# Gate and up weights streamed in memory order, with the column shuffle moved into the block transposes

## The chip, the cores and the metric

The kernel runs on one NeuronCore of a Trainium2 chip. TensorE (PE) multiplies matrices and writes PSUM; its weight loads are shown apart as PEld. VectorE (DVE) and ScalarE (ACT) do the elementwise work, GpSimd (POOL) prepares constants, and SyncE (SP) issues nearly all DMAs from HBM. The metric is device time in microseconds (us), as the median of several executions. A profile is one further execution with the hardware profiler on.

## The reference, cut to what matters

A decode step for four tokens, with attention over a sliding window and a SwiGLU block, both fed by the same layer-normed input and added to the residual:

```
x = A_x                                   # [4, 1, 512] bf16
xn = layernorm(x)
q = (xn @ wq)                             # 32 heads of 128
k, v = last 4096 rows of the caches       # 4 batches x 8 kv heads, each used by 4 query heads
attn = softmax(q k^T / sqrt(128)) v @ wo
ffn  = (silu(xn @ w_gate) * (xn @ w_up)) @ w_down     # 512 -> 1792 -> 512
out = x + attn + ffn
```

Only the two products with `w_gate` and `w_up` (512 x 1792 each) and what reads them are touched by the change.

## The kernel before, in words

All five engines run programs written out by hand, each in its own block of the source, and they meet only at semaphores; no scheduler moves anything. The order on each engine is the order of its block.

SP issues the loads on one queue: `wq`, two K tiles, `w_gate`, `w_up`, and then in turn a V tile and a K tile (2 MB each) as their buffers come free. Sixteen steps (`ND`) cover the cache, each with two batches' halves of one kv head. After the last K tile come `w_down`, the last V tile in two halves with semaphores of their own (`d_v[1]` and `d_vz`), and then `wo` in four pieces cut at 16, 26, 30 and 32 blocks (`WO_CUTS`). `w_gate` and `w_up` have been in SBUF since the start.

PE transposes K through PSUM, multiplies it with q, applies the softmax shift, and multiplies P with V; DVE evacuates the transposes and finds the row maxima. That is the loop. After the loop PE does, in this order: the second half of the last-but-one P times V (`pv(0, 1, ...)`), the last softmax shift, **the gate and up products (L443 to L449 of the source)**, the residual (`I4w` times `X`), the last two halves of P times V (which wait for the two halves of V), the down projection (which waits for `guT` from DVE), four transposes of the attention output, a small product that regroups it (`rep`), and the output projection with `wo`, 64 matmuls which wait for the four pieces of `wo` at blocks 0, 16, 26 and 30. DVE casts the sum and SP and ACT each store half of it.

The gate and up products put the 4 tokens (padded to 32) on the output partitions. Each of the four 32-partition groups `j` of PSUM takes 448 of the 1792 columns, and four input chunks `c` are summed, so that each product is 16 matmuls: 4 sets of 4 matmuls, one per column group of the array. Column number `f` of the weight is `14*p + t`: `w_down` is loaded so that row `f` sits in partition `p`, block `t`. The matmuls of before read each group's columns with `t` outermost, that is one element every 14, so that the 448 results lie in PSUM as 14 runs of 32, ready for 32x32 blocks:

```
wv = w[:, c, :].rearrange("p (m t) -> p t m", t=NF)
mm(o[32*j:32*j+32, :].rearrange("p (t m) -> p t m", t=NF), XnT[:, c, :], wv[:, :, 32*j:32*j+32], ...)
```

DVE then transposes each product in 32x32 blocks from PSUM to SBUF (`gT` at L330, `uT` at L332), which puts `p` on the partitions. ACT takes exp of `-gT` (L265), DVE makes silu(gate) times up (L334 to L340) into `guT`, and the down projection reads that. `norm` (L310 to L314) of the last attention step comes behind `guT` on DVE.

All these matmuls are issued through the helper `mm`, so their line in the profile is L354, and they are told apart by their tensors.

Of the kernel before, what the change touches and what calls it, by code (L numbers as in the profile page):

```python
# [10 lines left out]
def bass_parallel_sum__sliding_block_cached__swiglu_ffn__decode_kernel(  # L11
# [10 lines left out]
    out: bass.AP,  # L22
):
    B, _, D = A_x.shape
    _, HKV, Sk, Dh = A_k_cache.shape
    HQ = A_wq.shape[1] // Dh
    F = B_w_gate.shape[1]
# [3 lines left out]
    NF = F // 128  # L31
# [49 lines left out]
    XnT = sb("xnT", [128, NC, 32], BF16)  # L81
# [7 lines left out]
    gT = WQ[:, 0:NF * 64].bitcast(FP32)  # L89
    uT = WQ[:, NF * 64:NF * 128].bitcast(FP32)  # L90
# [16 lines left out]
    gate_ps = ps_kt[0][:, 0:NF * 32]  # L107
    up_ps = ps_kt[1][:, 0:NF * 32]
# [3 lines left out]
    def sem(name):  # L112
        return nc.alloc_semaphore(name=name)
# [21 lines left out]
    s_gt = sem("s_gt")  # L135
# [35 lines left out]
    with nc.Block() as block:  # L171
# [97 lines left out]
        @block.vector  # L269
        def _(eng):  # L270
            eng.wait_ge(d_x, 16)
            eng.tensor_reduce(st_neg[:], X[:], AX.X, ALU.add, negate=True).then_inc(s_xc, 1)
            eng.wait_ge(s_ss, 1)
            eng.tensor_scalar(st_var[:], st_sum[:], 1.0 / D, EPS * D * D, ALU.mult, ALU.add).then_inc(s_var, 1)
            eng.wait_ge(s_std, 1)
            eng.reciprocal(st_rstd[:], st_std[:]).then_inc(s_rs, 1)
            eng.wait_ge(s_xT, 1)
            eng.wait_ge(s_const, 1)
            eng.tensor_copy(XnT[:, :, 0:B], xT_ps.rearrange("p (c b) -> p c b", b=B)).then_inc(s_xnT, 1)
            for n in range(2):  # L280
                eng.wait_ge(s_q, n + 1)
                eng.transpose(qT[:, 512 * n:512 * n + 512], ps_kt[n][:])  # L282
            eng.drain()
            for i in range(2):
                last = eng.tensor_copy(  # L285
                    QZ[:].rearrange("p (k i) c -> p k i c", i=2)[:, :, i, 0:C].rearrange("p k (m h) -> p k m h", m=2),
                    qT.rearrange("p (k h x) -> p k x h", h=REP, x=32)[:, :, 2 * i:2 * i + 2, :])
            last.then_inc(s_qz, 1)
            eng.engine_nop().then_inc(s_ev, NG)

            def evac(u, tr):
                for g in range(NG):
                    eng.wait_ge(s_tr, tr + g + 1)
                    eng.tensor_copy(KT[:, u * HKN + 1024 * g:u * HKN + 1024 * (g + 1)],  # L294
                                    kt_ps[g].rearrange("p a b -> p (a b)")).then_inc(s_ev, 1)

            def row_max(bank, n):
                eng.wait_ge(s_sc, n)
                eng.tensor_reduce(RM[:], ps_S[bank][:].rearrange("p (t c) -> p c t", c=C), AX.X,  # L299
                                  ALU.max).then_inc(s_rm, 1)  # L300

            def shift(n):
                eng.wait_ge(s_mt, n)
                eng.tensor_reduce(m8[:], mt_ps, AX.X, ALU.max)  # L304
                eng.drain()
                eng.tensor_scalar(Dg[:], I8[:], m8[:, 0:1], -1.0, ALU.mult, ALU.mult).then_inc(s_dg, 1)

            def norm(n, b, r):
                eng.wait_ge(s_pv, n)
                eng.tensor_reduce(den[:], den_ps.rearrange("p (t c) -> p c t", c=C), AX.X, ALU.add)  # L310
                eng.drain()
                eng.reciprocal(den[:], den[:])
                eng.drain()
                eng.tensor_tensor(OT[:, 2 * b:2 * b + 2, ds(r * REP, REP)],  # L314
                                  O_ps.rearrange("p (j h) -> p j h", j=2),
                                  den[:].rearrange("p (j h) -> p j h", j=2), ALU.mult).then_inc(s_nrm, 1)

            with eng.Fori(0, ND // 2) as r:
                for b in range(2):
                    row_max(1 - b, 2 * r + (b + 1))  # L320
                    evac(0, 4 * NG * r + 2 * NG * b)
                    shift(2 * r + (b + 1))
                    norm(2 * r + (b + 1), b, r)
                    evac(1, 4 * NG * r + (2 * NG * b + NG))
            row_max(1, ND + 1)
            shift(ND + 1)
            norm(ND + 1, 0, ND // 2)

            eng.wait_ge(s_gate, 1)
            eng.transpose(gT, gate_ps).then_inc(s_gt, 1)  # L330
            eng.wait_ge(s_up, 1)
            eng.transpose(uT, up_ps)  # L332
            eng.wait_ge(s_ex, 1)
            eng.tensor_scalar(ex[:], ex[:], 1.0, None, ALU.add)  # L334
            eng.drain()
            eng.reciprocal(ex[:], ex[:])
            eng.drain()
            eng.tensor_tensor(ex[:], gT.rearrange("p (t b) -> p t b", b=32)[:, :, 0:B], ex[:], ALU.mult)
            eng.drain()
            eng.tensor_tensor(guT[:], uT.rearrange("p (t b) -> p t b", b=32)[:, :, 0:B], ex[:],  # L340
                              ALU.mult).then_inc(s_guT, 1)
            norm(ND + 2, 1, ND // 2)

            eng.wait_ge(s_t4, 1)
            eng.tensor_copy(OB[:], tr_ps).then_inc(s_ob, 1)  # L345
            eng.wait_ge(s_pm, 1)
            eng.tensor_copy(OP[:].rearrange("p c b -> p b c"), op_ps.rearrange("p (b c) -> p b c", b=B)).then_inc(s_op, 1)  # L347
            eng.wait_ge(s_acc, 1)
            eng.tensor_copy(y[:], ps_acc[:, 0:256]).then_inc(s_y, 1)  # L349

        @block.tensor
        def _(eng):
            def mm(o, l, r, start=False, stop=True):
                return eng.matmul(o, l, r, start=start, stop=stop, skip_group_check=True)  # L354
# [3 lines left out]
            for c in range(NC):  # L358
                last = eng.transpose(xT_ps[:, c * B:(c + 1) * B],  # L359
                                     xn[:].rearrange("b (p c) -> b c p", c=NC)[:, c, :], I4[:])  # L360
# [4 lines left out]
            for n in range(2):  # L365
                for c in range(NC):
                    wv = WQ[:, c * HQ * Dh:(c + 1) * HQ * Dh].rearrange("p (n h d) -> p n h d", n=2, d=Dh)
                    for j in range(4):
                        last = mm(ps_kt[n][32 * j:32 * j + 32, :].rearrange("p (h d) -> p h d", d=32), XnT[:, c, :],
                                  wv[:, n, :, 32 * j:32 * j + 32], start=(c == 0))  # L370
# [72 lines left out]
            for w, o, done, d in ((WG, gate_ps, s_gate, d_wg), (WU, up_ps, s_up, d_wu)):  # L443
                eng.wait_ge(d, 16)
                for c in range(NC):
                    wv = w[:, c, :].rearrange("p (m t) -> p t m", t=NF)
                    for j in range(4):
                        last = mm(o[32 * j:32 * j + 32, :].rearrange("p (t m) -> p t m", t=NF), XnT[:, c, :],
                                  wv[:, :, 32 * j:32 * j + 32], start=(c == 0))  # L449
                last.then_inc(done, 1)  # L450
            for n in range(2):
                mm(ps_acc[64 * n:64 * n + 64, 0:256], I4w[:], X[:, 256 * n:256 * n + 256], start=True)
# [9 lines left out]
            for i in range(B):  # L462
                last = eng.transpose(  # L463
                    tr_ps[:, i, :],
                    OT[:, i, REP:], ident[:])
            last.then_inc(s_t4, 1)
            eng.wait_ge(s_ob, 1)
            for e in range(REP):
                last = mm(op_ps.rearrange("p (b c) -> p b c", b=B), rep[:, e, :], OB[:, :, 32 * e:32 * e + 32],
                          start=(e == 0))  # L470
            last.then_inc(s_pm, 1)
            eng.wait_ge(s_op, 1)
            for c in range(NO):
                if c in WO_CUTS:
                    eng.wait_ge(d_wo[WO_CUTS.index(c)], 16)
                for n in range(2):
                    last = mm(ps_acc[64 * n:64 * n + B, 0:256], OP[:, c, :], WO[:, c, 256 * n:256 * n + 256])
# [29 lines left out]
```

## Time and profile before

| what | value |
|---|---|
| median of 3 runs | 200.13 us (199.88 to 200.15) |
| the profiled execution | 200.16 us, of which the span from first to last instruction is 198.4 us |
| PE busy | 167.4 us (84%) |
| DVE busy | 115.6 us (58%) |
| ACT busy | 16.6 us (8%) |
| HBM read | 81.01 MB, 408 GB/s over the span |

The page gives busy times per engine and a chain of work that ended last, followed back from the last instruction. An element count such as 128x448 is partitions by elements. A "timeline" row is start, duration, engine, line and operation, output and input tensors, count, and in brackets the idle time before it and what ended it. The tensor names are the kernel's; gate and up are `ps_kt<-wg_sb,xnT` and `ps_kt<-wu_sb,xnT`, because they use two of the PSUM banks of the K transposes, and `gT` and `uT` lie in the space of `wq_sb`.

### The profile page before, as it was taken

The page shows a single profiled execution, that of the slowest core. Times are in us where ns is not written, and L with a number is a line of the kernel's source. Part 1 is how long each engine was busy: PE and PEld are TensorE (multiplying, and loading weights), DVE is VectorE, ACT ScalarE, POOL GpSimd, SP SyncE. Part 2 cuts the span into 40 slices and gives each one's busy share as a digit, 9 for nine tenths or more (in the row PEclk, how much of TensorE's full clock was granted, in tenths as well). Part 3 has the DMA queues.
Part 4 walks back from the last instruction along what each step waited for, and adds up shares of the span by engine and source line. Part 5 has one row for each costly group of instructions (what it writes and reads, how often), then busy time and mean ns, then how long its engine had stood idle before and what let it go on. Part 6 is the DMA issues. An engine that isn't in the chain of part 4 may idle for free.

```text
span 198.4 us, 7741 instructions
## 1 busy us (share of the span) xinstructions
PE 167.4 (84%) x3458; PEld 141.5 (71%) x3458; DVE 115.6 (58%) x250; ACT 16.6 (8%) x26; POOL 10.3 (5%) x23
## 2 busy tenths in 40 slices
PE   0137999749999989898989898989898998989975
PEld 0113898748988878787878797978787887873363
DVE  1004758545777767676666767575858575762430
ACT  5600010001010101010101010101010101011000
POOL 8920000000000000000000000000000000000000
PEclk9999999988999999999999999999999999999999
DMA  6999999999999999999999999999999999999950
GB/s 232 449 410 426 432 419 430 438 423 433 406 433 423 429 429 429 443 436 423 429 429 426 433 446 426 429 429 426 433 446 426 429 429 426 436 418 448 411 230 1
DMA packets 5934, 81.10 MB, mean 409 GB/s; under 512 B 668, under 2 KB 680, under 8 KB 936
## 3 DMA queue, kind: packets, MB, share of 16 engines
q1 hardware_dynamic: 5912, 81.01, 95.9%
q8 instruction: 5, 0.08, 0.1%
q10 hardware_dynamic: 16, 0.01, 0.0%
q14 instruction: 1, 0.01, 0.0%
HBM read 81.01 MB, written 0.00 MB: 408 GB/s over the span
## 4 chain that ended last, share of the span: by engine, by line
DMA 51%; PE 42%; DVE 3%; issue 2%; DVEq 0%
DMA kbuf<-in_A_k_cache_dram 45%; PE ps_kt L382 17%; PE ps_s L354 9%; PE ps_o L354 7%; DMA wq_sb<-in_A_wq_dram 6%; PE ps_kt L354 5%; PE ps_acc L354 4%; DVE kT L294 1%; DVE kT L282 0%; DVE rm L299 0%; DVE oP L347 0%; DVE y_sb L349 0%; DVE oB L345 0%; DVE qz L285 0%; PE ps_kt L463 0%
## 5 line engine op out<-in xcount | busy, mean ns | idle before, releaser
L294 DVE COPY kT<-ps_kt 128x1024 bf16<-128x1024 bf16 x128 | 80.1, 684 | 27.2 <-PE ps_kt L382 27.1
L382 PE MATMUL ps_kt<-ident,kbuf 128*128 128x128 bf16 x1024 | 65.6, 224 | 10.6 <-DMA kbuf<-in_A_k_cache_dram 10.5
L382 PEld LDWEIGHTS ps_kt<-ident,kbuf 128*128 128x128 bf16 x1024 | 59.9, 100 | 15.9 <-issue 15.9
L354 PE MATMUL ps_o<-p,vbuf 128*128 128x64 bf16 x1120 | 38.7, 194 | 0.0
L354 PEld LDWEIGHTS ps_o<-p,vbuf 128*128 128x128 bf16 x1120 | 35.5, 98 | 1.2
L354 PEld LDWEIGHTS ps_s<-qz,kT 128*128 128x128 bf16 x1024 | 31.4, 98 | 6.7 <-issue 3.7
L354 PE MATMUL ps_s<-qz,kT 128*128 x1024 | 34.7, 192 | 1.2
L263 ACT ACTIVATE p<-ps_s 128x512 bf16<-128x512 f32 x17 | 10.1, 597 | 162.2 <-PE ps_s L354 162.2
L299 DVE TENSOR_REDUCE rm<-ps_s 128x8 bf16<-128x512 f32 x17 | 11.8, 692 | 20.5 <-PE ps_s L354 20.5
L354 PE MATMUL ps_o<-p,ones 128*128 128x128 bf16 (+1 forms) x69 | 7.0, 222 | 2.3 <-DVE qz L285 1.3
L354 PE MATMUL ps_kt<-wq_sb,xnT 128*32 128x512 bf16 x32 | 3.6, 630 | 5.4 <-DMA wq_sb<-in_A_wq_dram 5.4
L354 PEld LDWEIGHTS ps_o<-p,ones 128*128 128x128 bf16 x69 | 4.5, 98 | 3.5 <-issue 2.2
L359 PE MATMUL ps_acc<-i,xn 4*128 4x4 f32 x4 | 0.6, 254 | 7.4 <-ACT xn L260 7.4
L354 PE MATMUL ps_s<-mkc,mkr 2*128 2x512 bf16 x17 | 6.8, 398 | 0.0
L354 PE MATMUL ps_s<-dg,ones 8*128 8x512 bf16 x17 | 6.5, 385 | 0.0
L354 PEld LDWEIGHTS ps_kt<-wq_sb,xnT 128*32 128x32 bf16 x32 | 1.3, 139 | 6.9 <-issue 6.9
L282 DVE STREAM_TRANSPOSE kT<-ps_kt 128x512 f32<-128x512 f32 x2 | 1.4, 716 | 8.1 <-PE ps_kt L354 8.1
L310 DVE TENSOR_REDUCE den<-ps_o 128x8 f32<-128x128 f32 x18 | 5.0, 276 | 1.4 <-PE ps_o L354 1.4
L359 PEld LDWEIGHTS ps_acc<-i,xn 4*128 4x128 f32 x4 | 0.6, 208 | 7.3 <-issue 7.3
L207 POOL MEMSET vbuf<- 128x6144 f32 x1 | 5.2, 5222 | 0.0
L304 DVE TENSOR_REDUCE m<-ps_acc 8x1 f32<-8x128 f32 x17 | 4.6, 268 | 0.3 <-PE ps_acc L354 0.3
L314 DVE TENSOR_TENSOR oT<-ps_o,den 128x8 f32 (+1 forms) x18 | 3.0, 167 | 2.9 <-issue 2.7
(65 smaller groups left out, 52.0 us busy)
## 6 DMA issues: line engine op xcount, KB each, us to landing
kbuf<-in_A_k_cache_dram SPq DMA_DIRECT2D x16, 2048.0 KB, 12.6
vbuf<-in_A_v_cache_dram SPq DMA_DIRECT2D x15, 2048.0 KB, 11.2
wq_sb<-in_A_wq_dram SPq DMA_DIRECT2D x1, 4096.0 KB, 12.4
vbuf<-in_A_v_cache_dram SPq DMA_DIRECT2D x2, 1024.0 KB, 9.2
wo_sb<-in_A_wo_dram SPq DMA_DIRECT2D x1, 2048.0 KB, 14.5
wg_sb<-in_B_w_gate_dram SPq DMA_DIRECT2D x1, 1792.0 KB, 25.7
wu_sb<-in_B_w_up_dram SPq DMA_DIRECT2D x1, 1792.0 KB, 29.3
wd_sb<-in_B_w_down_dram SPq DMA_DIRECT2D x1, 1792.0 KB, 15.0
```

The costliest lines, as they stand in the source:

```text
L207: eng.memset(VB[:, HKN:].bitcast(FP32), 0.0)
L263: eng.activation(P[:, d % 2 * PS:d % 2 * PS + SN], ps_S[d % 2][:], ACT.Exp, scale=SCALE).then_inc(s_p, 1)
L282: eng.transpose(qT[:, 512 * n:512 * n + 512], ps_kt[n][:])
L294: eng.tensor_copy(KT[:, u * HKN + 1024 * g:u * HKN + 1024 * (g + 1)], kt_ps[g].rearrange("p a b -> p (a b)")).then_inc(s_ev, 1)
L299: eng.tensor_reduce(RM[:], ps_S[bank][:].rearrange("p (t c) -> p c t", c=C), AX.X, ALU.max).then_inc(s_rm, 1)
L304: eng.tensor_reduce(m8[:], mt_ps, AX.X, ALU.max)
L310: eng.tensor_reduce(den[:], den_ps.rearrange("p (t c) -> p c t", c=C), AX.X, ALU.add)
L314: eng.tensor_tensor(OT[:, 2 * b:2 * b + 2, ds(r * REP, REP)], O_ps.rearrange("p (j h) -> p j h", j=2), den[:].rearrange("p (j h) -> p j h" ...
L354: return eng.matmul(o, l, r, start=start, stop=stop, skip_group_check=True)
L359: last = eng.transpose(xT_ps[:, c * B:(c + 1) * B], xn[:].rearrange("b (p c) -> b c p", c=NC)[:, c, :], I4[:])
L382: last = eng.transpose(kt_ps[g][:, k, :], KB[:, a:a + 128], ident[:])
```

## The change

The matmuls read each group's 448 weight columns as they lie in memory, and write 448 results in that order. The 32x32 transposes read them back from PSUM in the order in which the matmuls wrote them before: for each block `t`, 32 fp32 values that lie 14 apart. Their output, and everything behind it, is as before. The number and order of the instructions on every engine is the same.

```diff
             eng.wait_ge(s_gate, 1)
-            eng.transpose(gT, gate_ps).then_inc(s_gt, 1)
+            eng.transpose(gT, gate_ps.rearrange("p (m t) -> p t m", t=NF)).then_inc(s_gt, 1)
             eng.wait_ge(s_up, 1)
-            eng.transpose(uT, up_ps)
+            eng.transpose(uT, up_ps.rearrange("p (m t) -> p t m", t=NF))
...
                 for c in range(NC):
-                    wv = w[:, c, :].rearrange("p (m t) -> p t m", t=NF)
                     for j in range(4):
-                        last = mm(o[32 * j:32 * j + 32, :].rearrange("p (t m) -> p t m", t=NF), XnT[:, c, :],
-                                  wv[:, :, 32 * j:32 * j + 32], start=(c == 0))
+                        last = mm(o[32 * j:32 * j + 32, :], XnT[:, c, :],
+                                  w[:, c, 32 * NF * j:32 * NF * (j + 1)], start=(c == 0))
                 last.then_inc(done, 1)
```

## The prediction

> **What bounds the kernel now.** I read the page first, then the chain in order of time, and the timeline of the last 20 us, where the changed lines lie. From the page:
>
> ```profile
> span 198.4 us, 7741 instructions
> DMA  6999999999999999999999999999999999999950
> ```
>
> The DMA engines are full until the last two of 40 slices, so most of the kernel is the stream from HBM. The end is another matter. The chain of work that ended last, in order of time (start, duration, what):
>
> ```profile
> 168.74 0.12 issue
> ...
> 180.23 6.57 PE ps_kt L354 x26
> 186.81 0.23 PE ps_acc L354 x2
> 187.03 2.20 PE ps_o L354 x68
> 189.23 1.62 PE ps_acc L354 x28
> 190.85 0.23 PE ps_kt L463 x4
> ...
> 192.50 3.68 PE ps_acc L354 x64
> 196.18 0.02 issue
> 196.20 0.42 DVE y_sb L349
> ```
>
> From 180.23 on PE never waits for a transfer: gate and up (6.57), residual, P times V, down projection, four transposes, and the output projection from 192.50. So here PE sets the end, and the change is in its longest piece. The timeline of that stretch:
>
> ```profile
> 180.16 3.42 PE L354 MATMUL ps_kt<-wg_sb,xnT 128*32 128x448 bf16 x16
> 183.38 3.43 PE L354 MATMUL ps_kt<-wu_sb,xnT 128*32 128x448 bf16 x16
> 183.62 0.65 DVE L330 STREAM_TRANSPOSE wq_sb<-ps_kt 128x448 f32<-128x448 f32 x1 [2.87 <-PE ps_kt L354]
> 184.31 0.25 ACT L265 ACTIVATE ex<-wq_sb 128x56 f32<-128x56 f32 x1 [3.45 <-DVE wq_sb L330]
> 186.74 0.29 PE L354 MATMUL ps_acc<-x_sb,i4w 4*64 4x256 bf16 x2
> 186.85 0.65 DVE L332 STREAM_TRANSPOSE wq_sb<-ps_kt 128x448 f32<-128x448 f32 x1 [2.57 <-PE ps_kt L354]
> 188.52 0.22 DVE L340 TENSOR_TENSOR guT<-wq_sb,ex 128x56 bf16<-128x56 f32 x1
> ```
>
> DVE's work on gate and up is hidden: guT is ready at 188.74, and PE reaches the down projection only at 189.16 to 189.23.
>
> What comes next behind PE is the stream. Issues of the last loads (first two rows), and their times to landing:
>
> ```profile
> 172.03 1.19 SPq L225 DMA_DIRECT2D vbuf<-in_A_v_cache_dram  x2
> 173.27 2.03 SPq L229 DMA_DIRECT2D wo_sb<-in_A_wo_dram  x4
> vbuf<-in_A_v_cache_dram SPq DMA_DIRECT2D x1, 1024.0 KB, 8.3
> vbuf<-in_A_v_cache_dram SPq DMA_DIRECT2D x1, 1024.0 KB, 10.1
> wo_sb<-in_A_wo_dram SPq DMA_DIRECT2D x1, 2048.0 KB, 14.5
> wo_sb<-in_A_wo_dram SPq DMA_DIRECT2D x1, 1280.0 KB, 16.9
> wo_sb<-in_A_wo_dram SPq DMA_DIRECT2D x1, 512.0 KB, 17.6
> wo_sb<-in_A_wo_dram SPq DMA_DIRECT2D x1, 256.0 KB, 17.8
> ```
>
> The halves of V are issued at 172.03 and about 172.64 and land at 180.3 and 182.7. Four wo issues fill 2.03 us, so they start at about 173.27, 173.9, 174.4 and 174.9, and the pieces land at 187.8, 190.8, 192.0 and 192.7. Their last use is at 195.8, three microseconds later. That 3 us is the room the change has.
>
> **The change part by part.**
>
> *The 32 matmuls on PE.* Four matmuls, one per column group, run side by side and make a set. Rows of the two products of this shape, and of PE's clock at the time of the first:
>
> ```profile
> L354 PE MATMUL ps_kt<-wg_sb,xnT 128*32 128x448 bf16 x16 | 3.4, 984 | 0.0
> 13.34 3.61 PE L354 MATMUL ps_kt<-wq_sb,xnT 128*32 128x512 bf16 x32 [5.37 <-DMA wq_sb<-in_A_wq_dram]
> L354 PE MATMUL ps_kt<-wq_sb,xnT 128*32 128x512 bf16 x32 | 3.6, 630 | 5.4 <-DMA wq_sb<-in_A_wq_dram 5.4
> 19.10 3.58 PE L382 MATMUL ps_kt<-ident,kbuf 128*128 128x128 bf16 x32
> 25.48 1.96 PE L382 MATMUL ps_kt<-ident,kbuf 128*128 128x128 bf16 x32
> ```
>
> Gate's 4 sets take (3.42 - 0.98)/3 = 0.81 us each, 1.8 ns per column. wq has the same form, but its moving operand is read in contiguous runs of 32: its 8 sets take (3.61 - 0.63)/7 = 0.43 us each, 0.83 ns per column, although PE was slow then: the same 32 transposes took 3.58 us at 19.10 and 1.96 at 25.48. At the later speed a set of 512 would take about half, 0.21, and one of 448 columns 0.43/2 x 448/512 = 0.19 us. Bounds: 0.19, and 0.81 (reading in order gains nothing). If wq was not slowed by the clock but by four streams at once, it is 0.43 x 448/512 = 0.37. I take 0.19, because the transposes behind wq show the clock; 0.37 changes nothing below. The 8 sets then take 1.5 us in place of 6.57: PE reaches the residual at 181.7 instead of 186.74, 5.0 us earlier.
>
> [...]
>
> *The two block transposes on DVE.* They were 0.65 us and read 448 contiguous fp32; now the step is 56 bytes. No row has a transpose from PSUM with a step. The nearest are reductions that read PSUM with a step of 8 fp32 (32 bytes), beside a contiguous transpose:
>
> ```profile
> L299 DVE TENSOR_REDUCE rm<-ps_s 128x8 bf16<-128x512 f32 x17 | 11.8, 692 | 20.5 <-PE ps_s L354 20.5
> L282 DVE STREAM_TRANSPOSE kT<-ps_kt 128x512 f32<-128x512 f32 x2 | 1.4, 716 | 8.1 <-PE ps_kt L354 8.1
> ```
>
> 512 elements at a step of 8 take 692 ns, 512 contiguous ones in a transpose 716. So a step costs nothing there; I take 0.65. The other end is PE's own ratio for the old read of SBUF, 0.81/0.19 = 4.3: 2.8 us each.
>
> [...]
>
> *DVE's chain.* gate is done at 180.16 + 0.75 + 0.24 (0.24 lies between the start of up and the gT transpose now: 183.38 to 183.62) = 181.15; gT ends 181.8, ACT's exp 182.1. up is done at about 181.85, uT ends 182.5, and guT 1.24 later (187.50 to 188.74 now), 183.75. norm of the last step follows on DVE as now, when P times V is done.
>
> *PE behind gate and up.* Residual at 181.7, first half of P times V from 182.15 to about 183.1 (its V half is there since 180.3); the second half needs V of 182.7, plus 0.12 which lies between a landing and PE's start (the first chain row), 182.8: not late. P times V ends 184.2, down projection at about 184.2 (guT 183.75 is ready), transposes at 185.6, wo at 192.50 - 5.05 = 187.45.
>
> *What is late next: wo.* The first piece is there at 187.8 + 0.1, so blocks 0 to 15 run from 187.9 to 189.6 (64 matmuls in 3.68 us less about 0.25 for the last one's end, 0.054 each). Then PE waits: block 16 at 190.9, block 26 at 192.1, block 30 at 192.75. The last four matmuls:
>
> ```profile
> 195.78 0.38 PE L354 MATMUL ps_acc<-wo_sb,oP 128*4 128x256 bf16 x4
> ```
>
> So DVE's cast starts at 192.75 + 0.38 + 0.04 = 193.17 instead of 196.20, 3.03 us earlier, and cast and stores are unchanged. Of 5.05 us that PE saves, 2.0 go into waiting for wo. Transfers do not move: all were issued by 175.3, before gate.
>
> *Sum.* 200.16 (profiled) - 3.03 = 197.13; the profiled execution (a span of 198.4 us and 1.8 us around it) is 0.03 over the median of the runs, so **197.1 us**. There are 2.0 us of cover on PE: the result stands with sets of up to 0.19 + 2.05/8 = 0.44 us. On DVE, guT may be 0.45 late before PE waits, so 2.4 us over both transposes, 1.8 us each, still cost nothing.
>
> **The rivals.**
>
> *PE's clock drops while it waits for wo.* Busy time and granted clock of two consecutive windows, and of the present tail (stretch, its length, PE busy and count, granted clock):
>
> ```profile
> 39.61:43.02 3.41, 0.71 (x17) 1.00 0.99 418
> 43.02:46.43 3.41, 3.41 (x40) 0.50 1.03 442
> ...
> 189.79:193.20 3.41, 2.37 (x42) 1.00 0.47 187
> ```
>
> After a window with 0.71 of 3.41 us busy the clock halved for one window; with 2.37 it did not. My forecast has PE busy 1.8 to 2.2 us in any 3.41 us from 184 to 193, between those and nearer to the latter. If it drops from about 190, blocks 16 to 25 take 20 x 0.107 = 2.1 us to 193.05, the last 12 matmuls 1.3 more, and the cast starts near 194.7: gain 1.5, **198.7 us**. [...]
>
> *The block transposes pay for the step.* At 2.8 us each gT ends 183.95, uT 186.75, guT 188.0; PE waits there, the down projection takes 1.62 and the steps to wo 1.65 (chain, 190.85 to 192.50), so wo starts at 188.05 + 3.27 = 191.3 and the end gains 1.2: **199.0 us**. Against it: the 692 ns row.
>
> *The same, on the other side.* The gain is gone when guT comes at 192.50 - 3.27 - 0.05 = 189.2, that is at +2.7 us or 3.35 us per transpose, 5 times now; at 8 times (5.2 us) guT comes at 192.85, and the time is **203.9 us**. No row shows a factor on DVE.
>
> *The change does not do what it says.* The slow sets come from four tiles sharing something and not from the step: sets stay 0.8, **200.1 us**. Against it: wq's 0.43 per set at a lower speed, in the same four tiles.
>
> **How the numbers follow.** Main case 0.78; clock drop 0.10; transposes near 2.8 us 0.07; transposes over 3.3 us 0.03; no change 0.02. For the main case wo's landings can move a few tenths: 196.7 to 197.5. The range is 196.7 to 198.8, which takes in the clock drop. No change means within 0.2%, 0.4 us, about what a measurement of this kernel can tell. Faster 0.94, same 0.03, slower 0.03.
>
> **What would show it.** Gate's 16 matmuls as one row of about 0.75 to 0.95 us in place of 3.42; L330 and L332 at 0.65 us; a new wait of PE's `ps_acc<-wo_sb,oP` for the DMA of wo_sb, about 1.2 us the longest, at block 16; DMA on the chain just ahead of the last matmuls; the cast at about 193.2. Wrong if L330 and L332 are far over 1.8 us, if the granted clock is under 1 in the last 6 us, or if wo lands later than 192.7.

## The result, and the profile after

The changed kernel took 197.16 us in the median of 4 runs (196.99 to 198.16), the kernel before 200.14 (199.88 to 200.25). The ratio is 0.986, with a 95% interval of 0.983 to 0.990. The forecast was 197.1 us, in a range of 196.7 to 198.8. The highest of the four times, 198.16, may be the clock rival's case, which is taken up below.

The profiled execution is the shortest of the four, 196.99 us, with a span of 195.2 us. Its timeline at the changed lines and behind them (start, duration, engine, line, operation, idle time before):

```profile
180.08 0.94 PE L354 MATMUL ps_kt<-wg_sb,xnT 128*32 128x448 bf16 x16
180.84 0.93 PE L354 MATMUL ps_kt<-wu_sb,xnT 128*32 128x448 bf16 x16
181.07 0.65 DVE L330 STREAM_TRANSPOSE wq_sb<-ps_kt 128x448 f32<-128x448 f32 x1 [0.40 <-PE ps_kt L354]
181.71 0.29 PE L354 MATMUL ps_acc<-x_sb,i4w 4*64 4x256 bf16 x2
181.83 0.65 DVE L332 STREAM_TRANSPOSE wq_sb<-ps_kt 128x448 f32<-128x448 f32 x1
183.50 0.22 DVE L340 TENSOR_TENSOR guT<-wq_sb,ex 128x56 bf16<-128x56 f32 x1
187.68 1.91 PE L354 MATMUL ps_acc<-wo_sb,oP 128*4 128x256 bf16 x32 [0.74 <-DMA wo_sb<-in_A_wo_dram]
190.69 2.22 PE L354 MATMUL ps_acc<-wo_sb,oP 128*4 128x256 bf16 x32 [1.09 <-DMA wo_sb<-in_A_wo_dram]
192.95 0.43 DVE L349 CAST y_sb<-ps_acc 128x256 bf16<-128x256 f32 x1 [5.53 <-PE ps_acc L354]
```

Gate and up shrank from 3.4 to 0.9 us each, and the block transposes still take 0.65. The residual starts at 181.71 instead of 186.74. Then the output projection, which ran through from 192.50 before, is broken up by waits for wo. The cast starts at 192.95 instead of 196.20.

The group of gate's matmuls (count, then busy us and mean ns), and of the last piece of wo (KB, us to landing):

```profile
L354 PE MATMUL ps_kt<-wg_sb,xnT 128*32 128x448 bf16 x16 | 0.9, 355 | 0.0
```

```profile
wo_sb<-in_A_wo_dram SPq DMA_DIRECT2D x1, 256.0 KB, 17.7
```

A set takes (0.94 - 0.355)/3 = 0.195 us. The chain that ended last now has a transfer in front of the end. First the page's shares, then the chain in order of time:

```profile
DMA 63%; PE 32%; issue 1%; DVE 1%; SPq 1%; DVEq 0%
```

```profile
173.83 16.82 DMA wo_sb<-in_A_wo_dram
190.64 0.04 issue
190.69 2.23 PE ps_acc L354 x32
192.92 0.03 issue
192.95 0.43 DVE y_sb L349
```

Before, the wait for V, wo and everything else loaded was hidden behind PE from 180.23 on, and DMA had 51% of the chain. Now wo is on it. (The chain follows the wait at block 16. PE then works through 20 matmuls, waits twice more for a short time, and does the last 8 and 4.)

### The profile page after: what moved, and what is told of

The parts are those of the page before. It is cut to its first block, busy times and chain, and to the rows that moved or that the text cites. A ratio compares the mean times of both kernels' runs of the same rounds, so it can differ in the third digit from the quotient of the medians.

```text
span 195.2 us, 7741 instructions
## 1 busy us (share of the span) xinstructions
PE 160.9 (82%) x3458; PEld 139.5 (71%) x3458; DVE 114.8 (59%) x250; ACT 16.6 (9%) x26; POOL 10.3 (5%) x23
## 4 chain that ended last, share of the span: by engine, by line
DMA 63%; PE 32%; issue 1%; DVE 1%; SPq 1%; DVEq 0%
DMA kbuf<-in_A_k_cache_dram 48%; PE ps_kt L382 16%; DMA wo_sb<-in_A_wo_dram 9%; PE ps_s L354 8%; DMA wq_sb<-in_A_wq_dram 6%; PE ps_o L354 5%; PE ps_kt L354 2%; PE ps_acc L354 2%; DVE kT L294 1%; SPq L225 1%; DVE kT L282 0%; SPq L229 0%; DVE y_sb L349 0%; DVE qz L285 0%; DVEq L293 0%
## 5 line engine op out<-in xcount | busy, mean ns | idle before, releaser
L382 PE MATMUL ps_kt<-ident,kbuf 128*128 128x128 bf16 x1024 | 62.8, 219 | 10.6 <-DMA kbuf<-in_A_k_cache_dram 10.6
L382 PEld LDWEIGHTS ps_kt<-ident,kbuf 128*128 128x128 bf16 x1024 | 57.3, 98 | 15.8 <-issue 15.7
L354 PEld LDWEIGHTS ps_s<-qz,kT 128*128 128x128 bf16 x1024 | 32.1, 99 | 6.7 <-issue 3.6
L354 PE MATMUL ps_s<-qz,kT 128*128 x1024 | 35.3, 193 | 1.2
L354 PE MATMUL ps_acc<-wo_sb,oP 128*4 128x256 bf16 x64 | 4.1, 272 | 1.8 <-DMA wo_sb<-in_A_wo_dram 1.8
L354 PEld LDWEIGHTS ps_acc<-wo_sb,oP 128*4 128x4 bf16 x64 | 2.5, 84 | 3.3 <-DMA wo_sb<-in_A_wo_dram 1.9
```

Source lines behind the costliest of these rows:

```text
L382: last = eng.transpose(kt_ps[g][:, k, :], KB[:, a:a + 128], ident[:])
```

## The experiments

**What the strided read costs: by steps.** The forecast priced one step only, 14. Two kernels read the 448 columns at other steps; the columns are then others, so that the products, and all behind them, are not those of the reference. For steps 4 and 8, in short form (2 and 7 in the other, in the same way):

```diff
-                        last = mm(o[32 * j:32 * j + 32, :], XnT[:, c, :],
-                                  w[:, c, 32 * NF * j:32 * NF * (j + 1)], start=(c == 0))
+                        # gate, step 4:
+                        wv = w[:, c, :].rearrange("p (m t) -> p t m", t=4)[:, j, :]
+                        # up, step 8:
+                        wv = w[:, c, :].rearrange("p (m t) -> p t m", t=8)[:, 2 * j:2 * j + 2, :]
+                        last = mm(o[32 * j:32 * j + 32, :], XnT[:, c, :], wv, start=(c == 0))
```

> The changed kernel with gate's 448 columns read at a step of 4 bf16 (8 bytes) and up's at a step of 8 (16 bytes), so that the products are of other columns. The set of four matmuls was 0.19 us at a step of 1 and 0.81 at 14. [...] Rival (cost grows with the bytes passed over, in proportion to 8, 16 and 28 bytes): gate 0.37 per set, up 0.55. The kernel: up late by 2.6 us against 2.0 us of cover, 197.7 us for the first, 197.2 for the rival.

> As the run at steps 4 and 8, with gate at a step of 2 bf16 (4 bytes) and up at a step of 7 (14 bytes). [...] Rival (in proportion to the bytes): gate 0.25, up 0.49. The kernel 197.1 to 197.5 us.

Timeline of both, first steps 4 and 8, then 2 and 7:

```profile
180.11 1.78 PE L354 MATMUL ps_kt<-wg_sb,xnT 128*32 128x448 bf16 x16
181.68 3.36 PE L354 MATMUL ps_kt<-wu_sb,xnT 128*32 128x448 bf16 x16
190.74 3.66 PE L354 MATMUL ps_acc<-wo_sb,oP 128*4 128x256 bf16 x64 [0.53 <-DVE oP L347]
```

```profile
180.08 0.98 PE L354 MATMUL ps_kt<-wg_sb,xnT 128*32 128x448 bf16 x16
180.88 2.95 PE L354 MATMUL ps_kt<-wu_sb,xnT 128*32 128x448 bf16 x16
```

The duration of one matmul in these rows, as least, median and most ns by tensor:

```profile
L354 PE MATMUL ps_kt<-wg_sb,xnT x16: 553/574/596, 180.1 to 181.3; 128*32 128x448 bf16 x16
L354 PE MATMUL ps_kt<-wu_sb,xnT x16: 965/967/969, 181.7 to 184.1; 128*32 128x448 bf16 x16
```

```profile
L354 PE MATMUL ps_kt<-wg_sb,xnT x16: 358/360/373, 180.1 to 180.7; 128*32 128x448 bf16 x16
L354 PE MATMUL ps_kt<-wu_sb,xnT x16: 852/867/869, 180.9 to 183.0; 128*32 128x448 bf16 x16
```

With the same subtraction as above, the sets are:

| step in bf16 | bytes | set, us | bytes over 16, at most 1 | 0.80 us times that |
|---|---|---|---|---|
| 1 | 2 | 0.195 | 1/8 | 0.10 |
| 2 | 4 | 0.21 | 1/4 | 0.20 |
| 4 | 8 | 0.40 | 1/2 | 0.40 |
| 7 | 14 | 0.69 | 7/8 | 0.70 |
| 8 | 16 | 0.80 | 1 | 0.80 |
| 14 | 28 | 0.81 | 1 | 0.80 |

At steps 4 and 8 neither expectation held: a step of 4 is not free (0.40 us against 0.195), and the cost does not go on growing with the bytes (0.80 us at 16, 0.81 at 28). What fits the six sets is 0.80 us times the step over 16 bytes, with 0.195 us, the set at a step of 1, as the floor: the cost grows in proportion up to 16 bytes, where it is 0.80 us/448 = 1.8 ns per column, and is the same at 28. A step of 8 bytes still costs half of that (0.40); at 4 bytes the step is nearly free (0.21 against 0.195). Step 3 and the steps between 16 and 28 bytes were not run, and the runs do not show what lies behind the fit.

The times were 198.53 us (steps 4 and 8) and 197.23 (2 and 7), one execution each. The first was to be 197.7 or, by the rival, 197.2. The 197.7 was reckoned with 0.19 per set for gate and 0.8 for up; no run shows 0.19 at a step of 4, and the sets measured were 0.40 and 0.80. The room was used up, and PE entered wo at 190.74, with no wait for a transfer.

**Whether the four column groups share the cost.** In the kernel before, all 16 gate matmuls went to one column group and up's to two; the sums are then not gate and up.

```diff
-            for w, o, done, d in ((WG, gate_ps, s_gate, d_wg), (WU, up_ps, s_up, d_wu)):
+            for w, o, done, d, k in ((WG, gate_ps, s_gate, d_wg, 1), (WU, up_ps, s_up, d_wu, 2)):
...
-                        last = mm(o[32 * j:32 * j + 32, :].rearrange("p (t m) -> p t m", t=NF), XnT[:, c, :],
-                                  wv[:, :, 32 * j:32 * j + 32], start=(c == 0))
+                        last = mm(o[32 * (j % k):32 * (j % k) + 32, :].rearrange("p (t m) -> p t m", t=NF),
+                                  XnT[:, c, :], wv[:, :, 32 * j:32 * j + 32], start=(c == 0 and j < k))
```

> The kernel before, with the same 32 matmuls and the same strided reads, but all of gate's in one column group (partitions 0 to 31 of the output) and all of up's in two. The sums are then not gate and up. Theory A (each strided read costs 4.3 times a contiguous one, whatever the other groups do): gate 16 x 0.8 = 12.9 us, up 8 x 0.8 = 6.5 us, and the kernel some 12 us longer. Theory B (four groups share one port that serves one strided column at a time, and so run one after another): 16 matmuls take 3.2 us however they are spread over groups, gate and up 3.2 to 3.4 us each, 200.1 us.

Timeline (14 of gate's 16, and 14 of up's), then two windows of PE busy time (length, busy and count, granted clock, DMA share and GB/s):

```profile
180.25 11.41 PE L354 MATMUL ps_kt<-wg_sb,xnT 128*32 128x448 bf16 x14
...
192.30 7.42 PE L354 MATMUL ps_kt<-wu_sb,xnT 128*32 128x448 bf16 x14
```

```profile
182.35:185.76 3.41, 3.41 (x5) 1.00 0.94 398
185.76:189.17 3.41, 3.41 (x6) 0.50 0.99 419
```

The time was 214.49 us, 14 us longer in the one execution, where theory A had 12. One group's matmuls start (11.41 - 0.98)/13 = 0.80 us apart, the same as a whole set of four before. So the cost is one of each stream's own reads, the four groups read side by side, and the rival that the change does nothing is out. From 180.25 to the residual at 199.65 PE takes 19.4 us, as theory A had it (12.9 and 6.5). Most of the rest comes behind that, where P times V takes 3.14 us from 200.40 instead of 2.03; the page gives the granted clock of the slice from 196.8 to 202.1 us as 7 tenths. The windows show two things more, which are taken up at the end.

**The step moved to PE's writes.** The matmuls read contiguously and write to PSUM at a step of 32 fp32; the transposes read contiguously. Against the changed kernel, with the second transpose (`uT`) changed in the same way:

```diff
-            eng.transpose(gT, gate_ps.rearrange("p (m t) -> p t m", t=NF)).then_inc(s_gt, 1)
+            eng.transpose(gT, gate_ps).then_inc(s_gt, 1)
...
-                        last = mm(o[32 * j:32 * j + 32, :], XnT[:, c, :],
-                                  w[:, c, 32 * NF * j:32 * NF * (j + 1)], start=(c == 0))
+                        last = mm(o[32 * j:32 * j + 32, :].rearrange("p (t m) -> p m t", t=NF), XnT[:, c, :],
+                                  w[:, c, 32 * NF * j:32 * NF * (j + 1)].rearrange("p (m t) -> p m t", t=NF),
+                                  start=(c == 0))
```

> The step moved to a third place: matmuls read the weights in memory order, but write their results to PSUM 32 fp32 apart (column 14m+t goes to place 32t+m), and the transposes read contiguously as in the kernel before. Theory (only PE's read of SBUF pays for a step): sets of 0.19 us as in the changed kernel, gate as one row of 0.95 us, 197.1 us. Rival (a step in PSUM slows matmuls as a step in SBUF does): sets of 0.8 us, gate 3.4 us, 200.1 us; anything between 0.44 and 0.8 us per set shows in the time, under 0.44 only in the row.

```profile
180.24 1.69 PE L354 MATMUL ps_kt<-wg_sb,xnT 128*32 128x448 bf16 x16
...
189.13 4.04 PE L354 MATMUL ps_acc<-wo_sb,oP 128*4 128x256 bf16 x64 [0.53 <-DVE oP L347]
```

```profile
L354 PE MATMUL ps_kt<-wg_sb,xnT x16: 549/581/581, 180.2 to 181.3; 128*32 128x448 bf16 x16
```

The set took (1.69 - 0.58)/3 = 0.37 us, between the two: at this one step in PSUM, 128 bytes, PE's writes run at about half rate. The time was 197.16 us (197.00 to 197.93), as for the changed kernel, since 0.37 is under the 0.44 us per set that the prediction's cover allows. It also shows the cover at work: wo starts 1.4 us later than in the changed kernel (189.13, 187.68) and the kernel ends at the same time.

**Whether the stream sets the end.** Only 7 of w_down's 14 blocks are loaded and each is used twice, in the changed kernel and in the kernel before; half of w_down is missing from the sum.

```diff
-            eng.dma_start(WD[:], wd_ap).then_inc(d_wd, 16)
+            eng.dma_start(WD[:, 0:NF // 2, :], wd_ap[:, 0:NF // 2, :]).then_inc(d_wd, 16)
...
-                    mm(ps_acc[64 * n:64 * n + B, 0:256], guT[:, t, :], WD[:, t, 256 * n:256 * n + 256])
+                    mm(ps_acc[64 * n:64 * n + B, 0:256], guT[:, t, :], WD[:, t % (NF // 2), 256 * n:256 * n + 256])
```

> The changed kernel with only the first 7 of the 14 blocks of w_down loaded, and used twice, so that the stream ahead of V and wo is 0.9 MB shorter, about 2.1 us at 430 GB/s; half of w_down is left out of the sum. Theory (the last piece of wo sets the end): wo lands 2.1 us earlier, PE hardly waits for it, and the time falls by up to 2.0 us to 195.1. Rival (PE's own chain or something else sets the end): 197.1 as without it.

> The same shorter load in the kernel before. Theory (there PE sets the end and wo lies ready 3 us ahead of its use): no change, 200.1 us. Rival (the stream sets the end in both): 198.0 us.

The output projection in the timeline of the changed kernel, then of the kernel before, with the shorter load:

```profile
187.43 3.66 PE L354 MATMUL ps_acc<-wo_sb,oP 128*4 128x256 bf16 x64 [0.53 <-DVE oP L347]
```

```profile
192.37 3.66 PE L354 MATMUL ps_acc<-wo_sb,oP 128*4 128x256 bf16 x64 [0.53 <-DVE oP L347]
```

The changed kernel fell to 195.19 us (195.08 to 195.88): its 64 matmuls run through without a wait for a transfer from 187.43, where the prediction had PE arrive (187.45). The kernel before stayed at 200.06 us, ratio 0.9995 (0.9985 to 1.0005). So the 2 us that PE saves and the time does not show are waiting for the stream, and before the change the stream did not set the end.

**Late executions, and PE's clock.** Of the changed kernel's first four executions one took 198.16 us, at a mean granted clock of 0.983 where the others had 0.990 or 0.991. The difference, 0.008, is about what one more window of 3.41 us at half clock, as in the kernel before from 43.02 to 46.43, would make (3.41/2/196 = 0.009). The kernel was run again, and once with matmuls added in the gaps:

```diff
+            def keep(n):
+                for _ in range(n):
+                    mm(ps_kt[0][:, 0:256], ident[:], P[:, 0:256], start=True)
...
             last.then_inc(s_t4, 1)
+            keep(4)
...
             last.then_inc(s_pm, 1)
+            keep(4)
...
                 if c in WO_CUTS:
+                    keep({0: 2, 16: 8, 26: 1, 30: 2}[c])
                     eng.wait_ge(d_wo[WO_CUTS.index(c)], 16)
```

> The changed kernel once more, to see how often it is slow: one of its four times was 198.16 us with a mean granted clock of 0.983, the other three 196.99 to 197.16 with 0.990 or 0.991. Theory (PE's clock halves for one window of 3.4 us while PE waits for wo; such a window is worth 3.4/2/196 = 0.009 of the mean clock): most runs 197.0 to 197.2 at 0.990 to 0.991, about one in four near 198.2 at 0.982 to 0.983. Rival (something from outside the core, that went by): no run above 197.5.

> The changed kernel with 21 more matmuls of 256 columns into a PSUM bank that nobody reads any more, 4 behind the transposes of the attention output, 4 behind the regrouping product and 2, 8, 1 and 2 ahead of the four waits for wo, where PE would be idle. Theory (clock halves because PE idles there): no run at a mean clock of 0.983, all 197.0 to 197.3. Rival (the slow run has another cause): as many slow runs as in e1. Should the extra matmuls not be hidden behind the wait for wo: at most 4 x 0.107 = 0.4 us later.

The repetition gave 197.30 in the median of 5 runs, one of them 198.25, again at 0.983. The four others had 0.991 or 0.974 with times of 197.04 to 197.34: in the one profiled at 0.974 the half clock lies at 36 to 47 us (0.53 in the mean of these), in the loop. With the added matmuls there was no execution at 0.983, but 197.90 us in the median of 6 (197.56 to 198.51). All six lie above the theory's 197.3: three by about the 0.4 us that was allowed for matmuls that are not hidden, and three are over 198, at 0.974 and 0.991. The profiled one was one of these, 198.19 us:

```profile
192.96 0.60 PE L354 MATMUL ps_acc<-wo_sb,oP 128*4 128x256 bf16 x8
193.49 0.39 PE L354 MATMUL ps_kt<-p,ident 128*128 128x256 bf16 x2
193.81 0.38 PE L354 MATMUL ps_acc<-wo_sb,oP 128*4 128x256 bf16 x4
194.24 0.42 DVE L349 CAST y_sb<-ps_acc 128x256 bf16<-128x256 f32 x1 [6.50 <-PE ps_acc L354]
```

```profile
wo_sb<-in_A_wo_dram SPq DMA_DIRECT2D x1, 256.0 KB, 18.2
```

```profile
L229 SPq DMA_DIRECT2D wo_sb<-in_A_wo_dram x4: 432/433/601, 173.5 to 175.1; - x4
```

PE is at full speed here (the last four matmuls take 0.38 us, as in the kernel before). The last piece lands at 175.1 + 18.2 = 193.3, where the changed kernel had about 192.5, and the added matmuls hold the last four up for another 0.4 us. So a late execution exists without a slow clock, with the stream late. Others had no lower mean clock either: 197.93 us in the run that writes to PSUM at a step, and 195.88 in the changed kernel with the shorter load, both at 0.991. Three more profiled executions of the changed kernel were to show where the lateness of such an execution lies:

> One more look at the changed kernel, for a profile of one of its late executions (some one in four so far, about 1 us late, in e2 and e3 at a mean clock no lower than that of the others). Theory now (the stream itself is later in such an execution, and since it sets the end, that passes through): in a late execution the last piece of wo lands 0.5 us or more after 192.8 and PE restarts 0.1 us behind it, at granted clock 1.00. Rival (PE's clock): the pieces land as in the other profiles, and the matmuls behind them run at 0.5. A look at an execution near 197.1 tells neither.

> Another look at the changed kernel, for the same reason and with the same two expectations: in an execution near 198.2 us, late landings of wo at a full clock, or landings as usual and a halved clock behind them.

> A third look at the changed kernel, for the same reason and with the same two expectations: in an execution near 198.2 us, late landings of wo at a full clock, or landings as usual and a halved clock behind them.

They gave 197.09, 197.14 and 197.40, all at 0.991, and so settle nothing. In the third, the last matmuls start at 192.93 and not 192.5, behind a last piece that came some 0.4 us later, at full clock.

**Finer cuts of wo.** A version that was meant to be faster:

```diff
-    WO_CUTS = (0, 16, 26, 30, 32)
+    WO_CUTS = (0, 20, 28, 31, 32)
```

> The changed kernel with the pieces of wo cut at 20, 28 and 31 blocks in place of 16, 26 and 30, so that 2 matmuls and not 4 follow the last landing. The last landing does not move (the bytes are the same). Theory: 2 x 0.054 = 0.1 us earlier, 197.0 us, within what can be told from no change. Rival (larger first pieces keep PE waiting where it now works): later by up to the 12 matmuls of 20 to 31 that then run close to the end, 0.5 us, 197.6 us.

```profile
189.08 3.92 PE L354 MATMUL ps_acc<-wo_sb,oP 128*4 128x256 bf16 x64 [1.96 <-DMA wo_sb<-in_A_wo_dram]
```

The two lowest of six were 196.85 and 197.00 us. That is at most 0.14 under the changed kernel's lowest (196.99) and too little to tell from no change, as the theory had it. The other four were 198.13 to 198.41, beyond the 197.6 of the rival, three of them at a mean clock of 0.982 or 0.983; the median is 198.19 and the ratio to the kernel before 0.989 (0.987 to 0.991). It is no improvement.

The idle time ahead of wo is 1.96 us here and was 0.74 (0.53 of either is the wait for `oP`, as in the runs with the shorter load). Three of 6 executions at the lower mean clock, against 2 of 12 of the changed kernel, are too few to call a difference. But the traces show how it could come about. In the emptiest stretch of 3.41 us near the end PE is busy for 0.94 us here (185.80 to 189.21), for 1.91 in the changed kernel (187.00 to 190.41) and for 2.37 in the kernel before. In the loop a full clock was halved after a window with 0.71 us busy in the kernel before (39.61 to 43.02) and after one with 0.46 in the changed kernel (34.55 to 37.96). Where the windows lie differs from one execution to the next: the first half clock begins at 43.02 us in the kernel before, at 37.96 in the changed kernel and, worked out from its mean clock of 0.84 from 23 to 43 us, at about 36.6 in its repetition. In the profiled execution of this variant the clock stayed full behind the empty stretch: the page gives 9 tenths or more in every slice from 49 us on.

Taken together, of 18 executions of the changed kernel and of this variant 5 had a mean clock lower by one window (0.982 or 0.983 against 0.991), all of them among the 6 that were late; the sixth, at 0.991, may have the late stream. That the window lies in the tail was not seen in a profile. Nor is a wait for wo needed for such an execution: of 35 executions of the kernel before that were run beside these experiments, two had 0.983, and with 200.60 and 200.68 us they are its two longest.

## Why the prediction was right

*The matmuls.* Forecast 0.19 us per set from wq at half speed; measured 0.195. The profile's record of the granted clock is 1.00 from 13 to 23 us, where wq ran, so it does not show the slow clock; the forecast read it from the transposes alone. The run with the added matmuls bears that out: its granted clock is 0.53 in the mean of 36 to 47 us, and 32 such transposes, from 42.32 us, took 3.59 us there, as against 3.58 behind wq. The residual was to start at 181.7 and started at 181.71. The higher bound for four streams at once (0.37) is refuted by the row, and the rival of no change by the one-group run: the cost follows the step and not the groups.

*The transposes.* Forecast 0.65 us each from the reductions at a step of 32 bytes; measured 0.65. The rivals with slow transposes are refuted by that: DVE pays nothing for 56 bytes in PSUM (0.65 us before and after). PE does pay for its writes at a step of 128 bytes in PSUM: 0.37 us per set against 0.195, a factor of 1.9.

*DVE's chain and PE behind it.* guT was to be ready at 183.75 and was at 183.72. PE would have reached wo at 187.45; the run with the shorter load shows 187.43.

*What is late next.* The wait at block 16 was to be the longest, 1.2 us, and is 1.09. The cast was to start at 193.17 and started at 192.95, because the last piece landed about 0.2 us sooner than the 192.7 of the forecast, at 174.8 + 17.7 = 192.5. The time is that landing plus four matmuls, the cast and the store. Two runs that change the load and not the work of PE separate this from the rest: 2 us off in the changed kernel, nothing off before.

*The clock rival.* It was given one chance in ten and 198.7 us. Times of 198.16 and 198.25, with a mean clock lower by one window, came in 2 of 12 executions of the changed kernel. If they are its case, the price was too high by half a microsecond: it had the drop begin at about 190 and slow all the last 32 matmuls, which no profile shows. That the lateness comes from that window is read from mean clocks and times, which went together in 5 of 5 cases of the changed kernel and its variant with finer cuts, and not from a trace; and the one late profile shows a late stream instead. Which of the two makes which late execution stays open.

## What to carry to other kernels

For a matmul's moving operand (the matrix that streams through the array, here bf16 weights) the step between columns decided: 1.8 ns per column at 16 and 28 bytes and half of that at 8, against 0.44 (0.195 us/448) in memory order. Put a shuffle where a run or a row shows the reader indifferent to steps, here DVE's read of PSUM (0.65 us in either order). Before forecasting the gain of a shorter piece on PE, read the landing times of what comes next: here 5.0 us off PE were worth 3.0, and the rest went into waiting. A price from another place in the same trace (wq) must be corrected for PE's speed there, which the same operation in two places gives away (32 transposes in 3.58 and in 1.96 us) even where the record of the clock does not (1.00 at both).

## What the runs showed of the hardware that was not expected

- The price of PE's strided read did not follow PE's clock. In the one-group run the granted clock went from 1.00 to 0.50 at 185.76 us, in the middle of gate, and the matmuls went on 0.80 us apart.
- The clock was halved there after a window in which the records show PE busy all the time (3.41 of 3.41 us). In the kernel before, four groups reading at the same step kept the full clock over the same records:

```profile
182.97:186.38 3.41, 3.41 (x20) 1.00 0.97 412
186.38:189.79 3.41, 3.41 (x86) 1.00 0.97 410
```

With up's two groups the one-group run shows both: the window from 192.59 to 196.00, at half clock, was followed by a full one, and the window from 196.00 to 199.41, at full clock, by a lower one (7 tenths in the slice from 196.8 to 202.1 us). So the busy time of a profile does not tell when the clock is halved: 3.41 us of it came before a halved window and before full ones. In the records the two kernels differ in the matmuls of such a window, 5 in the one-group run and 20 in the kernel before. What the clock follows was not shown.
- In the changed kernel the clock stayed full after a window with 2.33 us busy, and was halved after one with 1.34 us, when the work was over:

```profile
188.14:191.56 3.42, 2.33 (x45) 1.00 0.81 328
191.56:194.97 3.41, 1.34 (x20) 1.00 0.04 13
194.97:195.20 0.23, 0.00 (x0) 0.50 0.00 0
```

How much work in a window keeps the clock full is not fixed by these runs. In the traces of the two kernels, from 20 us on, windows with 0.46, 0.71 and 1.34 us busy came before a halved clock, and one with 2.16 (184.73 to 188.14 us in the changed kernel) before a full one; in the one-group run 3.41 was followed by a halved one.
